# The first expert unit, two tiles of the first four batches, computed block by block between the closing steps of attention

## The chip, the cores and the metric

One core of a Trainium2 chip runs the kernel. The metric is device time in microseconds, the median of three runs.

## The reference

Sparse attention over 8 batches, 8 heads and 576 tokens with 64 values a head (`scores` are scaled by 1/8; all but a row's 32 largest are dropped), then a mixture of 8 experts over the 4608 tokens, each sent to one expert:

```
scores = scale * np.matmul(q, k.transpose(0, 1, 3, 2))
kth = np.partition(scores, -top_k, axis=-1)[..., -top_k:-top_k + 1]
attn = softmax(np.where(scores >= kth, scores, -1e9))        # top_k = 32
x = (attn @ v).transpose(0, 2, 1, 3).reshape(4608, 512)
e = argmax(x @ w_gate)                                       # 8 experts
out[token] = gate[token] * (relu(x[token] @ w1[e]) @ w2[e])  # 512 -> 1024 -> 512
```

## The kernel before, in words

**Attention** runs in 144 steps, one for a group of query rows, in a loop whose count goes to 150 because a step's stages lag: at loop count t the search for the 32nd largest (`topk`, DVE MAX8 and MATCH_REPLACE) works on step t, `softmax` (POOL adds, ACT signs) on step t-2, `transp` (PE transposes into the PSUM tile `tt`) on t-3, `exps` (ACT exponential out of `tt`) and `av` (PE, product with V) one loop count later. For t from 144 on there is no more search; these are the closing steps. Beside the steps run *jobs*, generators in lanes with due times, that advance as a step has room: preparing K and Q, summing and repairing rows (`sums`, `find`, `redo`, `patch`), writing a batch's rows to `xs` and its router logits to `lps` (`rows`), and routing a batch (`route`, `j_route`): it reads the logits `ll`, finds each token's expert (`hist`, `cum`, a rank by PE), and scatters token numbers and gate weights into `table`, whose slots start at `ebase`. In j_route, a batch after which an expert's early unit may be formed (`ahead`) also counts by PE how many slots are missing (`skip`), so that later tokens are put behind that unit's slots, and loads the unit's `ids`.

**Experts.** A *unit* is an expert and a number T of tiles of 128 tokens. `EARLY = ((4, 1, 2), (3, 4, 3))` lists early units: expert 0 with two tiles, from batches 0 to 4; experts 1 to 4 with three, from batches 0 to 5. Experts 5 to 7 have five tiles each, then come the remainders of the early ones and one spare tile. A unit has 8 blocks of 128 hidden values; block k loads raw w1 and w2 slices (`raw_w`), splits each into a high and a low part (`parts_w`: the high copy of w1 on ACT, that of w2 on DVE, the subtraction for w1 on DVE, for w2 on POOL), and runs `hidden(k)` (three products a sum: high by high, high by low, low by high) and `project(k-1)`. `turn_x` transposes a gathered tile into `xh` and `xl`. After a unit's last block ACT scales the sums with the gate weights and POOL sends the rows to `out` with one indirect store a tile.

Ahead of its end, attention already loads blocks 0 and 1 into buffers of the Q and K loads (`rq`, `rk`), gathers unit 0's two tiles (into `kt`) and splits both blocks; everything else of unit 0 comes after the last step: `moe()` begins with unit 0's `turn_x` and goes through all blocks in order, while the jobs of the last batches are advanced between them.

`MAIN` is 4, so `NB9` is 9 chunks of 128 columns; `tt` is then 1152 columns in three banks of 512. `ps` is the two-bank tile of the scores. `sb` are score buffers in SBUF, `qk0` to `qk2` the transposed Q and K.

Of the kernel before, what the change touches and what calls it, by code (L numbers as in the profile page):

```python
# [8 lines left out]
F32 = mybir.dt.float32  # L9
F32R = mybir.dt.float32r  # L10
# [13 lines left out]
CHUNKS = (11, 10)  # L24
A0, A1, A2, A3 = -4, 1, 2, 2
EARLY = ((4, 1, 2), (3, 4, 3))
LA = 3
# [11 lines left out]
TAIL = 1  # L39
TADV = 5  # L40
FREE = (1, 2, 3, 4, 5)
# [7 lines left out]
def attention_moe(ctx, tc, q, k, v, w_gate, w1, w2, out):  # L49
# [134 lines left out]
    def pair():  # L184
        return work.tile([128, 2, S], F32, name="sb", bufs=SBUFS)
# [114 lines left out]
    NB9 = 2 * MAIN + 1  # L300
    three = psum.tile([128, NB9 * 128], F32, name="tt")

# [154 lines left out]
    def transp(t):  # L457
        x = EX[t].rearrange("p a s -> p (a s)")
        tt = three.rearrange("p (c q) -> p c q", c=NB9)
        for c in range(NB9):  # L460
            nc.tensor.matmul(tt[:, c], x[:, c * 128:(c + 1) * 128], ident, start=True, stop=True,  # L461
                             is_transpose=True)

    def exps(t):
        ET[t] = work.tile([128, NB9, 128], F32, name="et")
        assert t // NT in SHIFTED
        nc.scalar.activation(ET[t], three.rearrange("p (c q) -> p c q", c=NB9), AF.Exp, bias=shift[:, t // NT, 0:1],  # L467
                             scale=0.125)
# [320 lines left out]
    def j_route(b):  # L789
# [158 lines left out]

    def parts_w(k, tiles):
        W[k] = []  # L950
        for i, r in enumerate(RAW.pop(k)):
            hi, lo = tiles[2 * i:2 * i + 2]
            if i == 0:
                nc.scalar.activation(hi, r, AF.Copy)  # L954
            else:
                nc.vector.tensor_copy(hi, r)  # L956
            (nc.gpsimd if i else nc.vector).tensor_tensor(lo, r, hi, op=OP.subtract)  # L957
            W[k] += [w.rearrange("p (c f) -> p c f", c=DC) if i == 0 else w for w in (hi, lo)]


    def ahead_load(k):
        r = work.tile([128, MAIN, 4, D], F32, name=("rq", "rk")[k], bufs=1).rearrange("p i g d -> p (i g d)")
        raw_w(k, r[:, 0:DM], r[:, DM:2 * DM])

    def ahead_take():
        c, T = part_of[0]
        GX[0] = [jobs.tile([128, DM], F32, name="kt", bufs=4)[:, 0:DM] for _ in range(T)]
        for i in range(T):
            take(GX[0][i], ID[0][:, i, 0:1], c)

    def ahead_split(k):
        if k == 0:
            for i in range(2):
                t = jobs.tile([128, 2, VW], F32R, name=f"rv{(NQ + i) % NV}", bufs=1).rearrange("p g x -> p (g x)")
                SPARE.extend(t[:, c * DM:(c + 1) * DM] for c in range(2 * VW // DM))
            SPARE.extend(jobs.tile([128, DM], F32, name="kt", bufs=4).bitcast(F32R)[:, 0:DM] for _ in range(2))
        parts_w(k, [SPARE.pop(0) for _ in range(4)])

    SPARE = []
    prep(0)  # L980
# [16 lines left out]
    if NQ > 1:  # L997
        load_qk(1)
    load_v(0)
    prep(2)  # L1000
    AHEAD = [(A0, ahead_load, (0,)), (A0, ahead_load, (1,)), (A1, ahead_take, ()), (A2, ahead_split, (0,)),
             (A3, ahead_split, (1,))]
    delayed = None
    for t in range(steps + LAG + TD + 4):
# [60 lines left out]
        for at, job, a in AHEAD if first else ():  # L1065
            if t - steps == at:
                job(*a)
        m = t - LAG - TD - 3
# [12 lines left out]
    att_open[0] = False  # L1081
    while first and part_of[0][0] not in ROUTED or held[0]:
        advance(None)
        for queue in (gq, pq, aq, dq):
            flush(queue)
# [5 lines left out]
    ps_a = moe_pools.enter_context(tc.tile_pool(name="ps_a", bufs=1, space=PSUM, reuse_waits="tile"))  # L1091
    late = {}
    XP, HT, PY = {}, {}, {}
    outs = []

    def pool_of(u):
        return moe_a if u < first else late["sb"]
# [28 lines left out]

    def turn_x(u, t):
        T = units[u][2]
        if t >= T:
            return  # L1130
        p = pool_of(u)
        if t == 0:
            XP[u] = [p.tile([128, DC, T * 128], F32R, name=n, bufs=2) for n in ("xh", "xl2")]
        xh, xl = XP[u]
        s = slice(t * 128, (t + 1) * 128)
        pt = ps_a.tile([128, DC, 128], F32, name="mt") if u or not t else \
            ps_a.tile([128, 512], F32, name="ph", bufs=2).rearrange("p (c x) -> p c x", c=DC)
        for c in range(DC):
            nc.tensor.transpose(pt[:, c, :], GX[u][t][:, c * 128:(c + 1) * 128], ident)  # L1139
        nc.scalar.activation(xh[:, :, s], pt, AF.Copy)  # L1140
        nc.vector.tensor_tensor(xl[:, :, s], pt, xh[:, :, s], op=OP.subtract)

    def hidden(k):
        u, f = divmod(k, FC)
        T = units[u][2]
        xh, xl = XP[u]
        h1, l1 = W[k][0:2]
        p = pool_of(u)
        hh = p.tile([128, T * 128], F32R, name="hh", bufs=2)
        hl_ = p.tile([128, T * 128], F32R, name="hl", bufs=2)  # L1150
        HT[k] = (hh, hl_)
        nh = 1 if T <= 4 else 2
        w = T * 128 // nh
        for n in range(nh):
            s = slice(n * w, (n + 1) * w)
            ph = ps_a.tile([128, 512], F32, name="ph", bufs=2)[:, 0:w]
            seq = [(c, a, x) for c in range(DC) for a, x in ((h1, xh), (h1, xl), (l1, xh))]
            for m, (c, a, x) in enumerate(seq):
                nc.tensor.matmul(ph, a[:, c, :], x[:, c, s], start=(m == 0), stop=(m == len(seq) - 1))  # L1159
            nc.scalar.activation(hh[:, s], ph, AF.Relu)  # L1160
            nc.vector.scalar_tensor_tensor(hl_[:, s], ph, 0.0, hh[:, s], op0=OP.max, op1=OP.subtract)  # L1161

    def project(k):
        u, f = divmod(k, FC)
        T = units[u][2]
        hh, hl_ = HT.pop(k)
        h2, l2 = W.pop(k)[2:4]
        for t in range(T):
            if f == 0:
                p = ps_a if t < 3 else late["ps"]  # L1170
                PY[u, t] = p.tile([128, DM], F32, name=f"y{t}")
            s = slice(t * 128, (t + 1) * 128)
            for m, (a, x) in enumerate(((hh, h2), (hh, l2), (hl_, h2))):
                nc.tensor.matmul(PY[u, t], a[:, s], x, start=(f == 0 and m == 0), stop=(f == FC - 1 and m == 2))  # L1174
        if f == FC - 1:
            for t in range(T):
                y = pool_of(u).tile([128, DM], F32, name="yo", bufs=3 if u < first else 5)
                nc.scalar.activation(y, PY[u, t], AF.Copy, scale=ID[u][:, t, 2:3].bitcast(F32))  # L1178
                nc.gpsimd.memset(spacer, 0.0)
                st = nc.gpsimd.indirect_dma_start(  # L1180
                    out=out, out_offset=bass.IndirectOffsetOnAxis(ap=ID[u][:, t, 1:2], axis=0),
                    in_=y, in_offset=None, bounds_check=N - 1, oob_is_err=False)
                for o in outs:
                    tc.declare_no_dep(st.ins, o.ins, reason="each token has a row of its own")
                outs.append(st)

    def moe():
        K = len(units) * FC
        got, turned = set(), set()

# [4 lines left out]

        for k in range(2):
            load_w(k)
        while first == 0 and not late:
            yield
        if first:  # L1200
            got.add(0)
        fetch(0)
        load_w(2)
        if not first:
            split_w(0)
            split_w(1)
        for t in range(CT):
            turn_x(0, t)
        turned.add(0)
        for k in range(K):  # L1210
            u, f = divmod(k, FC)
# [10 lines left out]
            split_w(k + 2)  # L1222
            if k:
                project(k - 1)
# [272 lines left out]
```

## Time and profile before

| | us |
|---|---|
| median of 3 runs | 1303.01 (1302.87 to 1304.35) |
| profiled execution | 1301.19, its span 1299.4 |
| PE busy | 1217.2 (94%) |
| DVE busy | 1020.2 (79%) |
| ACT, POOL busy | 828.3 (64%), 830.7 (64%) |
| mean granted TensorE clock | 0.983 of full |

The page divides the span into 40 slices of 32.5 us and gives each engine's busy share in tenths; in the row of the granted clock two slices near 750 to 810 us stand below their neighbours, and DVE's row falls there from 9 to lower digits, where attention ends. A table by stretch gives the same for any two times. A timeline lists each instruction or run of like instructions with its start, its length, and in brackets how long its engine sat idle before it and what ended that. A line number is that of the kernel before; L265 is the helper through which all jobs record.

### The profile page before, as it was taken

The page shows a single profiled execution, that of the slowest core. Times are in us where ns is not written, and L with a number is a line of the kernel's source. Part 1 is how long each engine was busy: PE and PEld are TensorE (multiplying, and loading weights), DVE is VectorE, ACT ScalarE, POOL GpSimd, SP SyncE. Part 2 cuts the span into 40 slices and gives each one's busy share as a digit, 9 for nine tenths or more (in the row PEclk, how much of TensorE's full clock was granted, in tenths as well). Part 3 has the DMA queues.
Part 4 walks back from the last instruction along what each step waited for, and adds up shares of the span by engine and source line. Part 5 has one row for each costly group of instructions (what it writes and reads, how often), then busy time and mean ns, then how long its engine had stood idle before and what let it go on. Part 6 is the DMA issues. An engine that isn't in the chain of part 4 may idle for free.

```text
span 1299.4 us, 31672 instructions
## 1 busy us (share of the span) xinstructions
PE 1217.2 (94%) x9126; PEld 968.9 (75%) x9126; DVE 1020.2 (79%) x6889; ACT 828.3 (64%) x1691; POOL 830.7 (64%) x1205
## 2 busy tenths in 40 slices
PE   6999999999999999999998869999999999999997
PEld 3667667676666666667666658889899899989996
DVE  7999999999999999999998965746663333345664
ACT  4999798898888888888987843333332323233432
POOL 4676766867867867868957866676552424155654
PEclk8999999999999999999999978999999999999999
DMA  6765565655655656556653615646563434256774
GB/s 174 224 184 178 169 187 161 186 171 160 193 161 156 195 168 171 179 170 171 188 166 113 194 39 159 187 122 199 146 184 110 125 93 132 74 162 189 224 212 125
DMA packets 271239, 211.18 MB, mean 163 GB/s; under 512 B 136216, under 2 KB 214216, under 8 KB 271056
## 3 DMA queue, kind: packets, MB, share of 16 engines
q1 hardware_dynamic: 260320, 185.92, 48.2%
q0 software_dynamic: 9504, 22.86, 5.6%
q8 instruction: 74, 1.21, 0.4%
q14 instruction: 109, 0.89, 0.2%
q10 hardware_dynamic: 1232, 0.30, 0.1%
HBM read 102.49 MB, written 107.90 MB: 162 GB/s over the span
## 4 chain that ended last, share of the span: by engine, by line
DVE 43%; PE 43%; ACT 4%; issue 3%; POOL 3%; DMA 2%; SPq 1%; POOLq 0%; ACTq 0%; DVEq 0%
DVE cand L1025 21%; PE ph L1159 18%; PE y L1174 17%; DVE cand L1033 9%; DVE vq L1033 7%; PE pt L265 2%; ACT sg L454 2%; POOL sb L455 2%; PE mt L1139 1%; PE ps L367 1%; PE px L477 1%; PE tt L461 1%; DVE xm L265 1%; ACT et L467 1%; DMA rk<-in_k_dram 1%
## 5 line engine op out<-in xcount | busy, mean ns | idle before, releaser
L455 POOL TENSOR_TENSOR sb<-sb,sg 128x576 f32<-128x576 f32 x288 | 369.4, 1299 | 49.4 <-ACT sg L454 42.3
L1025 DVE MAX8 cand<-sb 128x8 f32<-128x52 f32 (+2 forms) x3024 | 368.3, 207 | 0.2 <-issue 0.2
L957 POOL TENSOR_TENSOR wl<-r,wh 128x512 fp32r<-128x512 f32 x110 | 142.4, 1294 | 220.8 <-DVE wh L956 213.5
L454 ACT ACTIVATE sg<-sb,nb 128x576 int8<-128x576 f32 x288 | 229.0, 795 | 63.0 <-POOL sb L455 63.0
L477 PEld LDWEIGHTS px<-et,rv 128*64 128x64 f32 x2688 | 130.9, 138 | 123.1 <-ACT xt L265 49.4
L1160 ACT ACTIVATE hh<-ph 128x320 fp32r<-128x320 f32 (+3 forms) x136 | 58.2, 428 | 241.6 <-PE ph L1159 240.1
L1033 DVE MAX8 vq<-cand 128x8 f32<-128x22 f32 (+7 forms) x1152 | 200.5, 205 | 0.0
L461 PE MATMUL tt<-turner,sb 128*128 128x128 f32 x1296 | 176.8, 278 | 23.0 <-POOL sb L455 19.9
L367 PE MATMUL ps<-qk 64*128 64x512 f32 (+1 forms) x576 | 184.9, 650 | 4.2 <-ACT sb L369 3.5
L1161 DVE SCALAR_TENSOR_TENSOR hl<-ph,hh 128x320 fp32r<-128x320 f32 (+3 forms) x136 | 65.0, 478 | 151.3 <-ACT hh L1160 151.2
L467 ACT ACTIVATE et<-tt,shift 128x1152 f32<-128x1152 f32 x144 | 178.2, 1238 | 2.6 <-PE tt L461 2.6
L477 PE MATMUL px<-et,rv 128*64 128x128 f32 (+1 forms) x2688 | 164.3, 268 | 14.6 <-ACT xt L265 9.0
L461 PEld LDWEIGHTS tt<-turner,sb 128*128 128x128 f32 x1296 | 147.9, 144 | 34.7 <-POOL sb L455 30.2
L1159 PE MATMUL ph<-xh,wh 128*128 128x320 f32 (+3 forms) x536 | 168.5, 314 | 0.0
L1159 PE MATMUL ph<-xh,wl 128*128 128x320 f32 (+3 forms) x536 | 165.3, 308 | 0.0
L1159 PE MATMUL ph<-xl,wh 128*128 128x320 f32 (+3 forms) x536 | 165.1, 308 | 0.0
L1033 DVE MATCH_REPLACE8 cand<-vq,cand 128x22 f32<-128x22 f32 (+2 forms) x864 | 158.6, 189 | 0.0
L369 ACT ACTIVATE sb<-ps 128x1024 f32<-128x1024 f32 x144 | 149.0, 1035 | 9.4 <-PE ps L367 9.4
L1174 PE MATMUL y<-wh,hh 128*128 128x512 f32 x324 | 127.9, 395 | 1.9 <-ACT yo L1178 1.9
L1174 PE MATMUL y<-wh,hl 128*128 128x512 f32 x324 | 128.3, 396 | 0.0
L1174 PE MATMUL y<-wl,hh 128*128 128x512 f32 x324 | 128.1, 395 | 0.0
L957 DVE TENSOR_TENSOR wl<-r,wh 128x512 fp32r<-128x512 f32 x110 | 95.7, 870 | 11.4 <-ACT wh L954 7.1
(261 smaller groups left out, 2179.3 us busy)
## 6 DMA issues: line engine op xcount, KB each, us to landing
r<-in_moe_w_dram SPq DMA_DIRECT2D x220, 256.0 KB
sc<-sb SPq DMA_DIRECT2D x128, 288.0 KB
sc<-sb SPq DMA_DIRECT2D x128, 256.0 KB
rv<-in_v_dram SPq DMA_DIRECT2D x32, 256.0 KB
xs<-xm SPq DMA_DIRECT2D x16, 512.0 KB
rq<-in_q_dram SPq DMA_DIRECT2D x60, 128.0 KB
rk<-in_k_dram SPq DMA_DIRECT2D x60, 128.0 KB
sc<-sb SPq DMA_DIRECT2D x32, 144.0 KB
```

Of the source, the lines that this page charges most:

```text
L367: nc.tensor.matmul(MAINS[:, n], qk[:, 0, w], qk[:, 1, 2 * LEFT:], start=True, stop=True)
L369: nc.scalar.activation(bass.AP(EX[-1].tensor, EX[-1].offset, [list(EX[-1].ap[0]), [S + LEFT, 2], [1, M]]), MAINS, AF.Copy)
L454: nc.scalar.activation(upper(SG[i]), SB[u], AF.Sign, bias=nb[:, i, 1:2], accum_out=CNT[b][:, 2 * lt + i:2 * lt + i + 1])
L455: nc.gpsimd.tensor_tensor(SB[u], SB[u], SG[i], op=OP.add)
L461: nc.tensor.matmul(tt[:, c], x[:, c * 128:(c + 1) * 128], ident, start=True, stop=True, is_transpose=True)
L467: nc.scalar.activation(ET[t], three.rearrange("p (c q) -> p c q", c=NB9), AF.Exp, bias=shift[:, t // NT, 0:1], scale=0.125)
L477: yield lambda kb=kb, blk=blk: nc.tensor.matmul(px[h * 64:(h + 1) * 64], block(rv, p % 2, kb if kb < MAIN else MAIN + n, h), et[:, blk, q] ...
L957: (nc.gpsimd if i else nc.vector).tensor_tensor(lo, r, hi, op=OP.subtract)
L1025: one[m][0](*one[m][1])
L1033: f(*a)
L1159: nc.tensor.matmul(ph, a[:, c, :], x[:, c, s], start=(m == 0), stop=(m == len(seq) - 1))
L1174: nc.tensor.matmul(PY[u, t], a[:, s], x, start=(f == 0 and m == 0), stop=(f == FC - 1 and m == 2))
```

## The change

Unit 0 now takes its two tiles from the first four batches (0 to 3), a batch earlier; expert 1 becomes a unit of two tiles from batches 0 to 4, and experts 2 to 4 keep three from batches 0 to 5. The number of tiles and the list of unit sizes stay, in another order. All of unit 0 is taken out of `moe()`, which starts at unit 1 (block 8), and goes into a generator `filler()`. It is called once at the end of each of the loop counts 140 to 144, for the loads, gathers, splits and transposes, and from count 145 on once a step, between `softmax` and `av`, for one block: hidden(k), project(k-1), the split of block k+2, the load of block k+4. What is left of it runs behind the loop. Its buffers are those of the scores: the split weights lie in `qk0` to `qk2` and score buffers, x and the hidden values in score buffers, the y sums in `ps`, the hidden sums in the 384 columns by which `tt` is widened. All of its subtractions run on DVE. `TADV`, the number of closing counts in which the jobs advance, goes from 5 to 7. Batch 3 has become a batch with `skip`, and its five table scatters keep their spacing.

```
-EARLY = ((4, 1, 2), (3, 4, 3))
+EARLY = ((5, 1, 2), (4, 1, 2), (3, 3, 3))
-TADV = 5
+TADV = 7
...
-    three = psum.tile([128, NB9 * 128], F32, name="tt")
+    three = psum.tile([128, 3 * 512], F32, name="tt")
...
-            if c == 0 or b not in ahead:
+            if c == 0 or b not in ahead or b == part_of[0][0]:
                 yield need(pool=1.0)
...
+    def filler():
+        T = units[0][2]
+        w = T * 128
+        for k in range(2):
+            ahead_load(k)
+        yield
+        yield
+        ahead_take(0, "kt", DM)
+        yield
+        flat = [work.tile([128, 2, KW], F32, name=f"qk{i}", bufs=1).rearrange("p g x -> p (g x)") for i in range(3)]
+        sets = [halves(flat[0]) + halves(flat[1])]
+        parts_w(0, sets[0], nc.vector)
+        ahead_load(2)
+        XP[0] = [spare().bitcast(F32R)[:, 0:DC * w].rearrange("p (c x) -> p c x", c=DC) for _ in range(2)]
+        hs = spare().bitcast(F32R)
+        yield
+        for t in range(T):
+            turn_x(0, t, MAINS[:, t].rearrange("p (c x) -> p c x", c=DC))
+        sets.append(halves(flat[2]) + halves(spare()))
+        parts_w(1, sets[1], nc.vector)
+        ahead_load(3)
+        yield
+        ph = three[:, NB9 * 128:NB9 * 128 + w]
+        for k in range(FC):
+            h = hs[:, (k % 2) * 2 * w:(k % 2 + 1) * 2 * w]
+            hidden(k, (h[:, 0:w], h[:, w:2 * w], ph))
+            if k:
+                project(k - 1, MAINS)
...
+                parts_w(k + 2, sets[(k + 2) % 3], nc.vector)
...
+            if k + 4 < FC + 2:
+                ahead_load(k + 4)
+            if k >= FC - 3 and 1 not in GX and part_of[1][0] in ROUTED:
+                ahead_take(1, "xt", S)
+            yield
+        while part_of[1][0] not in ROUTED:
+            yield
+        if 1 not in GX:
+            ahead_take(1, "xt", S)
+        project(FC - 1, MAINS, spare())
...
+        if t > steps:
+            next(fills, None)
         if grp(t - LAG - TD - 2):
             av(t - LAG - TD - 2, grp(t - LAG - TD - 2))
...
+        if steps + A0 <= t <= steps:
+            next(fills)
...
-        for k in range(K):
+        for k in range(FC, K):
```

**PE, behind the search's last steps.** Before: from the rank of a batch's route (`hist`, `cum`) through av of steps 140 and 141 (the first two `px<-et` rows; `rv` is V) to the transposes of step 143.

```order
L265 MATMUL pt0_246<-hist_121,before_104 128x40
L265 MATMUL pt0_246<-cum_13209,ones_108 128x40
L477 MATMUL px_250<-et_13287,rv3_240 64x128 x8
L461 MATMUL tt_248<-turner_102,sb_12896 128x128 x9
L265 MATMUL pt0_246<-turner_102,r_sb_12616 128x128 x4
L477 MATMUL px_250<-et_13351,rv3_240 64x128 x8
L461 MATMUL tt_248<-turner_102,sb_12978 128x128 x9
```

The same place now. L978 are the transposes of `turn_x` (`kt` is a gathered tile), L1001 the matmuls of `hidden`, L1016 those of `project`.

```order
L265 MATMUL pt1_247<-hist_121,before_104 128x40
L265 MATMUL pt1_247<-cum_13215,ones_108 128x40
L978 MATMUL ps_249<-turner_102,kt_13216 128x128 x4
L978 MATMUL ps_249<-turner_102,kt_13217 128x128 x4
L1001 MATMUL tt_248<-sb_13308,qk0_13298 128x256
...
L477 MATMUL px_250<-et_13312,rv3_240 64x128 x8
L461 MATMUL tt_248<-turner_102,sb_12902 128x128 x9
L265 MATMUL pt1_247<-turner_102,r_sb_12622 128x128 x4
L1001 MATMUL tt_248<-sb_13308,qk2_13300 128x256
...
L1016 MATMUL ps_249<-qk1_13299,sb_13310 128x512 x6
L477 MATMUL px_250<-et_13396,rv3_240 64x128 x8
```

The transposes of unit 0 and hidden(0) have come between `cum` and av of step 140, hidden(1) and project(0) between av of steps 140 and 141.

**ACT, from unit 0 to unit 1.** In the changed kernel, with the queues and engines that each row waits for (DMASW are POOL's DMAs). L1002 writes the hidden values, L1021 the two scaled output tiles, L979 the copies `xh` of the next unit.

```order
L1002 ACTIVATE sb<-tt 128x256 [waits DVE_49,PE_49]
L954 ACTIVATE rv_13776<-rq 128x512 [waits DMAHW0_49]
L1002 ACTIVATE sb<-tt 128x256 [waits DVE_49,PE_49]
L954 ACTIVATE rv_13777<-rk 128x512 [waits DMAHW2_49]
L1021 ACTIVATE sb<-ps,ids_11146 128x512 [waits PE_49]
L1021 ACTIVATE sb<-ps,ids_11146 128x512
L979 ACTIVATE xh<-mt 128x4x128 [waits DMASW0_49,DMASW7_49,PE_49,Activation_49]
L979 ACTIVATE xh<-ph 128x4x128 [waits PE_49]
L1002 ACTIVATE hh<-ph 128x256 [waits DMAHW7_49,DVE_49,PE_49]
```

In the kernel before, the last outputs of unit 0 (L1178) stand behind a block of unit 1, and unit 1's copies (L1140) behind PE alone.

```order
L1140 ACTIVATE xh<-mt 128x4x128 [waits PE_49]
...
L1140 ACTIVATE xh<-mt 128x4x128 [waits PE_49]
...
L1160 ACTIVATE hh<-ph 128x256 [waits DVE_49,PE_49]
L954 ACTIVATE wh_13958<-r_13897 128x512 [waits DMAHW0_49]
...
L1160 ACTIVATE hh<-ph 128x384 [waits PE_49,Activation_49]
L954 ACTIVATE wh_13995<-r_13954 128x512 [waits DMAHW4_49]
L1178 ACTIVATE yo<-y_13634,ids_12353 128x512 [waits DMAHW3_49,PE_49]
L1178 ACTIVATE yo<-y_13638,ids_12353 128x512 [waits PE_49]
```

What moved: the copies of the next unit, which stood ahead of unit 0's last blocks, now stand behind unit 0's outputs and wait for two of POOL's DMAs; these are the two indirect stores of those outputs.

## Rows read from the trace of the kernel before

**Rows 1.** Stretch, us, busy us of PE, PEld, DVE, ACT, POOL; clock, DMA share, GB/s

```profile
762.00:786.00 24.00, 18.88 (x131) 15.38 (x131) 9.14 (x31) 9.29 (x18) 19.05 (x32) 0.77 0.26 67
```

**Rows 2.** The same view in shorter stretches, for the granted clock

```profile
770.00:776.00 6.00, 5.55 (x32) 4.98 (x33) 0.24 (x2) 2.74 (x7) 5.14 (x11) 0.50 0.32 88
...
788.00:794.00 6.00, 5.77 (x26) 5.64 (x27) 1.67 (x5) 1.36 (x4) 0.92 (x1) 0.53 0.37 116
```

**Rows 3.** Timeline of PE, closing steps: start, us, engine line op out<-in xcount [idle <-releaser]

```profile
761.77 0.23 PE L265 MATMUL pt<-hist,before 128*128 128x40 bf16 x1 [3.05 <-DVE hist L265]
...
762.40 1.97 PE L477 MATMUL px<-et,rv 128*64 128x128 f32 x16
...
770.45 1.97 PE L477 MATMUL px<-et,rv 128*64 128x128 f32 x16 [3.13 <-ACT r_et L265]
...
785.35 0.35 PE L265 MATMUL pt<-rhs,r_qx 128*128 128x2 bf16 x8 [1.73 <-DVE r_qx L265]
```

**Rows 4.** Timeline of DVE, same columns: the split of a block

```profile
775.87 0.69 DVE L957 TENSOR_TENSOR rv<-rq,rv 128x512 fp32r<-128x512 f32 x1 [5.76 <-ACT rv L954]
776.48 0.42 DVE L956 CAST rv<-rq 128x512 fp32r<-128x512 f32 x1
```

**Rows 5.** Timelines of ACT and POOL: an exponential, a gather

```profile
762.61 1.21 ACT L467 ACTIVATE et<-tt,shift 128x1152 f32<-128x1152 f32 x1
...
770.95 1.09 POOL L876 DMA_INDIRECT kt<-xs,ids  x1 [0.16 <-issue]
```

**Rows 6.** Timeline of PE: the first unit's blocks and what follows

```profile
785.59 0.63 PE L1139 MATMUL mt<-turner,kt 128*128 128x128 f32 x4
...
788.23 0.58 PE L1159 MATMUL ph<-xl,rv 128*128 128x256 f32 x1 [0.25 <-DVE xl L1141]
...
793.31 0.81 PE L1174 MATMUL y<-rv,hh 128*128 128x512 f32 x2
...
794.88 0.90 PE L265 MATMUL pt<-turner,xt 128*128 128x144 f32 x6
...
795.96 0.36 PE L1159 MATMUL ph<-xh,wh 128*128 128x256 f32 x1
...
797.48 0.63 PE L1174 MATMUL y<-kt,hh 128*128 128x512 f32 x2
...
817.17 0.33 PE L1159 MATMUL ph<-xh,wh 128*128 128x384 f32 x1
...
820.66 0.33 PE L1159 MATMUL ph<-xh,wh 128*128 128x384 f32 x1
...
824.82 0.50 PE L1174 MATMUL y<-wh,hh 128*128 128x512 f32 x1 [1.91 <-ACT yo L1178]
```

**Rows 7.** Timeline of ACT: xh, a wait for weights, two outputs

```profile
786.26 0.60 ACT L1140 ACTIVATE xh<-mt 128x512 fp32r<-128x512 f32 x1 [0.35 <-PE mt L1139]
...
823.56 0.63 ACT L954 ACTIVATE wh<-r 128x512 fp32r<-128x512 f32 x1 [3.26 <-DMA r<-in_moe_w_dram]
824.10 1.25 ACT L1178 ACTIVATE yo<-y,ids 128x512 f32<-128x512 f32 x2
```

**Rows 8.** All indirect stores of output rows: durations in ns, times to landing

```profile
L1180 POOL DMA_INDIRECT out_dram<-yo,ids x41: 981/1006/1452, 828.6 to 1291.9; - x41
...
DMA to landing us min/median/max: 2.6/3.7/6.0
```

**Rows 9.** Timelines around skip: DVE and PE at batch 4, both where batch 3's goes

```profile
706.66 0.16 DVE L265 TENSOR_SCALAR skip<-pt 128x1 f32<-128x1 f32 x1 [4.43 <-ACT sg L454]
...
707.37 0.57 DVE L265 TENSOR_TENSOR ebase<-ebase,skip 128x5 f32<-128x5 f32 x1
...
698.06 2.57 PE L461 MATMUL tt<-turner,sb 128*128 128x128 f32 x9 [4.66 <-POOL sb L455]
...
631.81 0.96 PE L265 MATMUL pt<-wg,r_et 128*128 128x8 f32 x8
...
634.24 0.17 DVE L1033 MATCH_REPLACE8 cand<-vq,cand 128x22 f32<-128x22 f32 x1
```

More of the change, by code (lines that the diff above doesn't have):

```diff
@@ L947, in raw_w, with parts_w @@
             nc.sync.dma_start(r2, w2[e, f * 128:(f + 1) * 128, :])
-    def parts_w(k, tiles):
+    def parts_w(k, tiles, other=None):
         W[k] = []
@@ L956, in parts_w, with turn_x @@
                 nc.vector.tensor_copy(hi, r)
-            (nc.gpsimd if i else nc.vector).tensor_tensor(lo, r, hi, op=OP.subtract)
+            ((other or nc.gpsimd) if i else nc.vector).tensor_tensor(lo, r, hi, op=OP.subtract)
             W[k] += [w.rearrange("p (c f) -> p c f", c=DC) if i == 0 else w for w in (hi, lo)]
+    late = {}
+    XP, HT, PY = {}, {}, {}
+    outs = []
+    def turn_x(u, t, pt=None):
+        T = units[u][2]
+        if t >= T:
+            return
+        if u not in XP:
+            p = pool_of(u)
+            XP[u] = [p.tile([128, DC, T * 128], F32R, name=n, bufs=2) for n in ("xh", "xl2")]
+        xh, xl = XP[u]
+        s = slice(t * 128, (t + 1) * 128)
+        if pt is None:
+            pt = ps_a.tile([128, DC, 128], F32, name="mt") if u > 1 or not t else \
+                ps_a.tile([128, 512], F32, name="ph", bufs=2).rearrange("p (c x) -> p c x", c=DC)
+        for c in range(DC):
+            nc.tensor.transpose(pt[:, c, :], GX[u][t][:, c * 128:(c + 1) * 128], ident)
+        nc.scalar.activation(xh[:, :, s], pt, AF.Copy)
+        nc.vector.tensor_tensor(xl[:, :, s], pt, xh[:, :, s], op=OP.subtract)
@@ new lines, in hidden @@
+    def hidden(k, tiles=None):
+        u, f = divmod(k, FC)
+        T = units[u][2]
+        xh, xl = XP[u]
+        h1, l1 = W[k][0:2]
+        if tiles:
+            hh, hl_, _ = tiles
+        else:
+            p = pool_of(u)
+            hh = p.tile([128, T * 128], F32R, name="hh", bufs=2)
+            hl_ = p.tile([128, T * 128], F32R, name="hl", bufs=2)
+        HT[k] = (hh, hl_)
+        nh = 1 if T <= 4 else 2
+        w = T * 128 // nh
+        for n in range(nh):
+            s = slice(n * w, (n + 1) * w)
+            ph = tiles[2] if tiles else ps_a.tile([128, 512], F32, name="ph", bufs=2)[:, 0:w]
+            seq = [(c, a, x) for c in range(DC) for a, x in ((h1, xh), (h1, xl), (l1, xh))]
+            for m, (c, a, x) in enumerate(seq):
+                nc.tensor.matmul(ph, a[:, c, :], x[:, c, s], start=(m == 0), stop=(m == len(seq) - 1))
+            nc.scalar.activation(hh[:, s], ph, AF.Relu)
+            nc.vector.scalar_tensor_tensor(hl_[:, s], ph, 0.0, hh[:, s], op0=OP.max, op1=OP.subtract)
@@ new lines, in project @@
+    def project(k, py=None, ys=None):
+        u, f = divmod(k, FC)
+        T = units[u][2]
+        hh, hl_ = HT.pop(k)
+        h2, l2 = W.pop(k)[2:4]
+        for t in range(T):
+            if f == 0:
+                PY[u, t] = py[:, t] if py is not None else \
+                    (ps_a if t < 3 else late["ps"]).tile([128, DM], F32, name=f"y{t}")
+            s = slice(t * 128, (t + 1) * 128)
+            for m, (a, x) in enumerate(((hh, h2), (hh, l2), (hl_, h2))):
+                nc.tensor.matmul(PY[u, t], a[:, s], x, start=(f == 0 and m == 0), stop=(f == FC - 1 and m == 2))
+        if f == FC - 1:
+            for t in range(T):
+                y = ys[:, t * DM:(t + 1) * DM] if ys is not None else \
+                    pool_of(u).tile([128, DM], F32, name="yo", bufs=3 if u < first else 5)
+                nc.scalar.activation(y, PY[u, t], AF.Copy, scale=ID[u][:, t, 2:3].bitcast(F32))
+                nc.gpsimd.memset(spacer, 0.0)
+                st = nc.gpsimd.indirect_dma_start(
+                    out=out, out_offset=bass.IndirectOffsetOnAxis(ap=ID[u][:, t, 1:2], axis=0),
+                    in_=y, in_offset=None, bounds_check=N - 1, oob_is_err=False)
+                for o in outs:
+                    tc.declare_no_dep(st.ins, o.ins, reason="each token has a row of its own")
+                outs.append(st)
@@ L968, in ahead_take @@
         for i in range(T):
[L969 to L977, printed above, removed]
@@ L1081, in attention_moe @@
     att_open[0] = False
-    while first and part_of[0][0] not in ROUTED or held[0]:
+    while held[0] or next(fills, fills) is not fills:
         advance(None)
@@ L1125, in gather @@
             take(GX[u][t], ID[u][:, t, 0:1], part_of[u][0] if u < first else None)
[L1127 to L1185, printed above, removed]
@@ L1187, in moe @@
     def moe():
         K = len(units) * FC
-        got, turned = set(), set()
+        got, turned = {0, 1}, {0}
         def fetch(u):
@@ L1194, in fetch @@
                 gather(u)
[L1196 to L1209, printed above, removed]
-        for k in range(K):
+        load_w(FC + 2)
+        for k in range(FC, K):
             u, f = divmod(k, FC)
```

43 lines of the change are left out of this document (26 added, 17 removed).

## The prediction

> **What bounds the kernel now.** I read the page's slices first, then a table by stretch, then the timelines of the single engines between the end of attention and the second expert unit. Until about 760 us DVE works without a pause on the top-32 search, and every DVE microsecond added there is added to the time. From 821 us to the end PE is the bound. Between the two lies the closing stretch, 762 to 786 us: PE is busy for 18.88 of 24 us, at a mean granted clock of 0.77 [rows 1]. So 5.1 us of PE stand idle there and the rest is partly slow. The idle time comes from waits: 3.05 us for hist, 3.13 us for r_et, 1.73 us for r_qx [rows 3]. Each is followed by a stretch at 0.50, the lower of TensorE's two levels, 1.2 GHz: 770 to 776 us directly after the wait for r_et, and 788 to 794 us at 0.53 [rows 2]. What the change can win is those 5.1 us and part of the slow clock. After the last patch matmul (the "mark" from here on, r_qx at 785.35) the first unit's eight blocks run: block 0's hidden layer from 788.23, and the whole unit is finished with the second unit's first block at 820.66 [rows 6].
>
> **What a block costs.** Two hidden layers at the half clock take 788.23 to 793.31, 2.55 us each; one at full clock takes 795.96 to 797.48, 1.5 us. A projection is six matmuls at 0.23 us, 1.4 us (797.48 to the next entry) [rows 6].
>
> **Part 1, main stage.** Batch 3 is now a batch whose routing also adjusts the slot base: one small matmul, three DVE operations, one 4 KB load. The load and the matmul lie beside other work. The DVE operations do not: 0.16 and 0.57 us and one as short as the first [rows 9], together 0.8 us after pipelining, on the engine that sets the time. At batch 4 the first of them also waited 4.43 us, because PE was late that step: it had itself waited 4.66 us for POOL. At batch 3's place PE has just finished the logits matmuls at 631.81 to 632.8, and DVE reaches the spot where skip is inserted at 634.4, so the operand is there before it [rows 9]. The bounds are 0.6 and 5 us; I take **+0.8**, the row nearest in place.
>
> **Part 2, the start of the closing stretch.** The split of block 0 is now on DVE ahead of hist: 0.61 us to the cast, 0.34 for it, 0.6 for the second subtraction (starts in [rows 4]), 1.55 us. PE's hist goes from 761.77 to about 763.3, its sum to 764.2. PE then does unit 0's transposes before av(140). Four transposes at the slow clock take 0.9 us, the copy xh 0.6 [rows 7], the subtraction 0.7; the second tile's transposes wait for the first tile's subtraction, because both lie in the one PSUM tile that the scores used. Twice 2.2 is 4.4 us: 768.6. ACT comes to the exponential of step 141 (1.21 us [rows 5]) only after both copies, so it ends near 769.5. Block 0's hidden sums go to the last third of the tile that this exponential reads, so hidden(0) starts at 769.5 and at half clock ends at 772.1. Only then comes av(140), which stood at 762.40 [rows 3]: **9.7 us late**. The two gathers of unit 0, 1.09 us of POOL each [rows 5], move into the last steps of attention, two steps ahead of what POOL's sums feed; I cost that at nothing, and at most 2.2 us if that lead is gone.
>
> Here a rule speaks for the wait. The trace has PE waiting 3.13 us for ACT to empty a tile that shares its bank with another job's output [rows 3]. The Trainium skill, "PSUM — Partial Sum Buffer", section "PSUM bank collisions raise a hardware error", says that two engines may not touch one bank and quadrant together even at different columns, so the exponential has to be out of the bank before hidden(0) begins; by columns alone hidden(0) would start 0.9 us sooner and the sum would be that much lower. The row agrees.
>
> **Part 3, to the mark.** From av(140) to the mark the kernel before needs 785.35 - 762.40 = 23 us with its 5.1 us of idle PE. The changed order puts hidden(1), (2), (3) and project(0), (1), (2) in between: 3 x 1.5 + 3 x 1.4 = 8.7 us at full clock. If these fill all the idle time the mark comes at 772.1 + 23 + 8.7 - 5.1 = **798.7**. I take neither a gain from a faster clock nor a loss from the further waits (each hidden layer waits for that step's exponential, each exponential for the splits of the step before); these have opposite signs. Bounds: were all of PE's added work, 10.2 us of blocks and 0.9 of transposes, laid into the holes and the slow stretch raised to full clock (18.88 x 0.23 = 4.3 us), the mark would be at 785.35 + 11.1 - 5.1 - 4.3 = 787. With the same six pieces at half clock (3 x 2.55 + 3 x 2.6 = 15.5) it would be 772.1 + 23 + 15.5 - 5.1 = 805.5.
>
> **Part 4, the rest of unit 0.** Behind the mark: four hidden layers and five projections, 6.0 + 7.0, and the patch jobs' matmuls between them. Before, 795.96 to 817.17 holds six hidden layers and six projections (17.4), three transposes of 0.43 and so 2.5 us of such jobs, and 1.08 us more stand at 794.88 [rows 6]: 3.6 us. The unit ends at 798.7 + 16.6 = 815.3.
>
> **Part 5, the hand-over, a new wait.** Unit 0's two output tiles are put into a score buffer, and the area where unit 1's xh lies covers it. Unit 1's first copy on ACT therefore waits for both indirect stores of the output. After project(7): one scaled copy 0.65 (two take 1.25 [rows 7]), some 0.3 to POOL's issue, 1.3 for the first store (1.0 us and its gap [rows 8]), then the second to landing 3.7 (median; 2.6 to 6.0 [rows 8]), two xh copies 1.0, one subtraction 0.7: **7.7 us** in which PE has nothing but the two transposes and what is queued behind them. hidden(8) begins at 823.0. Only by a page's figure: the Trainium skill, "DMA: Bandwidth & Descriptors", section "Anatomy of one DMA", gives about 2.0 us and the bytes over 436 GB/s, an estimate of 2.6 us for 256 KB, and the sum would be 1.1 us lower; the trace's least landing is that, its median is not [rows 8].
>
> Then TensorE falls to its lower level, as it did after 3.1 us of idling [rows 2, 3]. Priced by the stretch at 0.53: 6 x 0.47 = **2.8 us**.
>
> **Against the kernel before.** There 820.66 is reached with hidden(8) done (2.1 us, from 817.17) and about one transpose set more, so the same work lies behind it at 818.1. Behind that stood 1.91 us at 824.82, for weights whose load sat on SP behind a load of router logits (ACT waits 3.26 us for them [rows 6, 7]). In the changed kernel these weights have 7.7 idle microseconds to arrive, so this stall goes: 820.0 is to be compared. Difference: 823.0 - 820.0 + 2.8 + 0.8 = +6.6. Everything behind is the same number of tiles in units of the same sizes. The profiled execution took 1301.19 and so 1307.8 now; it lies 1.8 below the median of 1303.01, on which the forecast stands: 1309.6, given as **1309.5**.
>
> DVE has 9.14 of 24 us filled [rows 1]; eight splits of 1.55 over the 40 us of the unit do not make it the bound. The lanes that patch and route the last batches end later, at block 31 of 40, and the spare units still find their tokens.
>
> **Rivals.** A difference below 0.2%, 2.6 us, cannot be told from none here.
> *The holes are filled* (faster): PE's early blocks keep it from idling, the clock stays at its upper level through the closing stretch and the mark comes at 787 to 788. Then the sum is 11 lower: 1298.5. For it: 5.1 us of idle PE and a clock of 0.77. Against: the chains of single operations across PE, ACT and DVE in part 2, which put more waiting ahead of av(140). It decides where the mark lies ahead of about 789. Chance 0.13.
> *Half of it* (no change): the mark at 792 to 794, or the hand-over paid without a drop of the clock; 1302 to 1305. Chance 0.20.
> *Nothing overlaps* (slower still): each hidden layer waits for an exponential that waits for a split, the blocks run as a second string at the lower clock, and the mark stands at the upper bound of 805.5: 6.8 more, 1316.3. Chance 0.12.
> *skip stalls at batch 3 as at batch 4*: 4.4 us more, 1314. Against it stand the times of rows 9. Chance 0.08.
> The forecast, 1306 to 1313, keeps 0.47.
>
> **The numbers.** Slower is 0.47 + 0.12 + 0.08 = 0.67, same 0.20, faster 0.13. The range leaves out the far half of the faster case and the end of the one in which nothing overlaps: 1301 to 1316.
>
> **What would show it.** The mark (r_qx matmuls) near 798; av(140) ten microseconds later than before; a wait of PE on xh or on its transposes' copy of 6 to 7 us near 815 to 823, named by a DMA of the output, and a clock near 0.5 right behind it; no wait for weights at the second unit; skip's three operations near 634 without a wait. Wrong would be: a mark ahead of 790, PE at full clock from 762 to 786, a hand-over below 3 us, or DVE idle for microseconds before 757.

## The result and the profile after

The changed kernel takes 1314.63 us (median of 4 runs, 1313.59 to 1317.0), the kernel before 1302.94 on the same chips (1300.34 to 1304.35). The ratio is 1.0095 with a 95% interval of 1.0074 to 1.0116: 11.7 us slower, where 6.5 had been forecast. The profiled execution took 1317.0 with a span of 1314.7 and is the longest of the four.

The closing stretch by the same table as [rows 1]: start and end, length, busy us of PE, PE's weight loads, DVE, ACT and POOL, then the granted clock, DMA share and GB/s.

```profile
762.00:786.00 24.00, 13.35 (x89) 10.90 (x88) 15.54 (x45) 8.97 (x17) 10.64 (x16) 0.72 0.22 68
786.00:821.00 35.00, 33.16 (x241) 28.22 (x240) 17.28 (x38) 10.26 (x22) 19.79 (x36) 1.00 0.57 146
```

PE is not busier from 762 to 786 but less busy, 13.35 us against 18.88, and the clock is 0.72 against 0.77. DVE is busier, 15.54 against 9.14. Only the stretch behind it, 786 to 821, is better: a clock of 1.00 against 0.90 before.

The timeline of PE, as in [rows 3, 6]. The first line, the transposes of rinvl, is the last work of the search's steps.

```profile
761.55 0.35 PE L265 MATMUL pt<-rinvl,turner 128*64 128x1 f32 x8
766.76 0.23 PE L265 MATMUL pt<-hist,before 128*128 128x40 bf16 x1 [4.87 <-DVE hist L265]
...
773.28 2.93 PE L1001 MATMUL tt<-sb,qk 128*128 128x256 f32 x12 [2.31 <-ACT et L467]
776.14 1.97 PE L477 MATMUL px<-et,rv 128*64 128x128 f32 x16
...
801.38 0.34 PE L265 MATMUL pt<-rhs,r_qx 128*128 128x2 bf16 x8
...
816.94 1.66 PE L1016 MATMUL ps<-sb 128*128 128x512 f32 x6
...
826.85 0.58 PE L1001 MATMUL ph<-xh,rv 128*128 128x256 f32 x1 [7.38 <-ACT xh L979]
...
832.69 0.62 PE L1016 MATMUL y<-rv,hh 128*128 128x512 f32 x2
```

In the kernel before the same instruction stood here:

```profile
758.37 0.35 PE L265 MATMUL pt<-rinvl,turner 128*64 128x1 f32 x8
```

All of PE's closing work is best counted from that line. The changed profile lies 3.18 us later at it (761.55 against 758.37). From there av(140) comes 14.6 us later, at 776.14, where it came 4.0 us later before (762.40 [rows 3]); the mark 39.8 us later (801.38) instead of 27.0; unit 0's last projection (it starts at 816.94) gives way to unit 1's transposes at 818.44, 56.9 us behind that line. Then PE stands for 7.38 us and starts unit 1 at 826.85, and the first two hidden layers there take until 832.69, 5.84 us instead of 3.0.

The table by stretch between these places, first the kernel before (rinvl to av(140), av(140) to the mark), then the changed one:

```profile
758.37:762.40 4.03, 0.72 (x14) 0.46 (x10) 3.96 (x20) 0.49 (x3) 2.31 (x3) 0.65 0.06 13
762.40:785.35 22.95, 18.09 (x119) 14.73 (x118) 8.59 (x28) 9.12 (x17) 18.00 (x32) 0.76 0.25 66
```

```profile
761.55:776.14 14.59, 5.67 (x34) 4.52 (x30) 9.62 (x29) 4.73 (x10) 5.74 (x5) 0.59 0.19 55
776.14:801.38 25.24, 23.09 (x172) 18.67 (x172) 12.76 (x34) 8.60 (x16) 13.54 (x28) 0.96 0.43 106
```

Ahead of av(140) PE now stands idle for 8.9 us (14.59 - 5.67) instead of 3.3. Behind it, up to the mark, it is idle for 2.2 us instead of 4.9 and runs at 0.96 of the clock instead of 0.76. So the blocks did fill the holes behind av(140), but larger ones opened ahead of it.

The waits of PE from 740 us to the end (what waited, for what, us in total, how often, the longest):

```profile
PE tt L1001 <- ACT et L467: 4.2, 2, 2.3
PE y L1016 <- DVE hl L1003: 3.2, 1, 3.2
...
PE mt L978 <- DMA gx<-xs,ids: 1.8, 2, 1.5
```

The first belongs to hidden(0) and hidden(1), which wait for an exponential. The other two lie behind unit 0: 3.2 us for hl at 953, and 1.8 for the gathered tiles of unit 2.

ACT and POOL at the hand-over:

```profile
818.63 1.26 ACT L1021 ACTIVATE sb<-ps,ids 128x512 f32<-128x512 f32 x2 [3.15 <-PE ps L1016]
825.71 0.60 ACT L979 ACTIVATE xh<-mt 128x512 fp32r<-128x512 f32 x1 [5.81 <-DMA out_dram<-sb,ids]
```

```profile
820.97 0.97 POOL L1023 DMA_INDIRECT out_dram<-sb,ids  x1 [0.21 <-issue]
```

The second store was issued at 820.97 and xh could be written at 825.71, 4.7 us later; ACT's row names the stores as what ended its wait.

The second stall comes at the plan of the spare tile (the small operations that make the table of the last tiles), a place that the prediction did not price. POOL, DVE and PE there, and the granted clock behind it:

```profile
945.32 0.99 POOL L876 DMA_INDIRECT gx<-xs,ids  x1
...
951.38 0.19 POOL L1296 IOTA tl_i<- 128x44 f32 x1
```

```profile
951.61 0.19 DVE L1301 TENSOR_SCALAR tr<-tl_i 128x44 f32<-128x44 f32 x1 [7.75 <-issue]
```

```profile
953.23 0.79 PE L1016 MATMUL y<-wh,hl 128*128 128x512 f32 x1 [3.19 <-DVE hl L1003]
```

```profile
950.00:955.00 5.00, 1.81 (x5) 1.49 (x5) 3.25 (x10) 0.62 (x2) 2.07 (x4) 0.71 0.51 155
955.00:960.00 5.00, 5.00 (x20) 4.50 (x20) 3.88 (x11) 0.60 (x1) 1.74 (x2) 0.61 0.57 161
```

POOL issues the five gathers of a five-tile unit from 945.32 on, and only then the iota that the plan starts from (951.38). DVE stands idle for 7.75 us; its row names no releaser, but the operation reads what the iota writes and starts as that ends (951.57). The hl of a block is queued behind it; PE waits 3.19 us for that hl, and runs ten microseconds at 0.71 and 0.61. In the kernel before the same operation of DVE waited 0.21 us:

```profile
927.25 0.19 DVE L1261 TENSOR_SCALAR tr<-tl_i 128x44 f32<-128x44 f32 x1 [0.21 <-POOL tl_i L1256]
```

DVE in the main stage, a wait and batch 3's skip:

```profile
DVE skip L265 <- PE pt L265: 5.3, 1, 5.3
```

```profile
635.64 0.14 DVE L265 TENSOR_SCALAR skip<-pt 128x1 f32<-128x1 f32 x1
```

skip at batch 3 has no wait, as forecast. The wait for skip at batch 4 is 0.9 us longer than in the profile of before [rows 9]; one for mm (part of a batch's shift), between 100 and 200 us, takes 3.5 us against 1.5. The latter is not the change: in the kernels whose code up to there is that of the changed one it lies anywhere between 1.1 and 3.8 us. The two make up most of the 3.18 us by which this profile is late at the first line.

### The profile page after: what moved, and what is told of

The parts are those of the page before. It is cut to its first block, busy times and chain, and to the rows that moved or that the text cites. A ratio compares the mean times of both kernels' runs of the same rounds, so it can differ in the third digit from the quotient of the medians.

```text
span 1314.7 us, 31668 instructions
## 1 busy us (share of the span) xinstructions
PE 1219.1 (93%) x9127; PEld 968.9 (74%) x9127; DVE 1016.1 (77%) x6902; ACT 827.6 (63%) x1691; POOL 821.6 (62%) x1194
## 4 chain that ended last, share of the span: by engine, by line
DVE 47%; PE 39%; issue 5%; POOL 3%; ACT 3%; DMA 2%; SPq 1%; POOLq 0%; ACTq 0%; DVEq 0%
DVE cand L1143 23%; PE ph L1001 16%; PE y L1016 15%; DVE cand L1151 10%; DVE vq L1151 8%; PE pt L265 2%; PE px L477 1%; PE ps L367 1%; PE mt L978 1%; DVE xm L265 1%; PE tt L461 1%; ACT sg L454 1%; DMA rk<-in_k_dram 1%; ACT et L467 1%; SPq L113 1%
## 5 line engine op out<-in xcount | busy, mean ns | idle before, releaser
L957 POOL TENSOR_TENSOR wl<-r,wh 128x512 fp32r<-128x512 f32 x102 | 131.8, 1293 | 228.2 <-DVE wh L956 220.8
L454 ACT ACTIVATE sg<-sb,nb 128x576 int8<-128x576 f32 x288 | 228.6, 794 | 61.4 <-POOL sb L455 60.5
L1002 ACT ACTIVATE hh<-ph 128x320 fp32r<-128x320 f32 (+3 forms) x128 | 55.2, 431 | 236.2 <-PE ph L1001 225.0
L1003 DVE SCALAR_TENSOR_TENSOR hl<-ph,hh 128x320 fp32r<-128x320 f32 (+3 forms) x128 | 61.6, 481 | 149.5 <-ACT hh L1002 142.1
L1001 PE MATMUL ph<-xh,wh 128*128 128x320 f32 (+3 forms) x504 | 159.3, 316 | 0.0
L1001 PE MATMUL ph<-xh,wl 128*128 128x320 f32 (+3 forms) x504 | 155.8, 309 | 0.0
L1001 PE MATMUL ph<-xl,wh 128*128 128x320 f32 (+3 forms) x504 | 155.8, 309 | 0.0
L1016 PE MATMUL y<-wh,hl 128*128 128x512 f32 x308 | 122.0, 396 | 3.2 <-DVE hl L1003 3.2
L1016 PE MATMUL y<-wl,hh 128*128 128x512 f32 x308 | 121.7, 395 | 0.0
L1016 PE MATMUL y<-wh,hh 128*128 128x512 f32 x308 | 121.1, 393 | 0.0
L1001 PEld LDWEIGHTS ph<-xh,wh 128*128 128x128 f32 x504 | 95.1, 189 | 5.6 <-issue 2.6
```

The costliest lines, as they stand in the source:

```text
L454: nc.scalar.activation(upper(SG[i]), SB[u], AF.Sign, bias=nb[:, i, 1:2], accum_out=CNT[b][:, 2 * lt + i:2 * lt + i + 1])
L957: ((other or nc.gpsimd) if i else nc.vector).tensor_tensor(lo, r, hi, op=OP.subtract)
```

## The experiments

All ratios are against runs of the kernel before on the same chip.

### The outputs of unit 0 in other buffers

```
-                y = ys[:, t * DM:(t + 1) * DM] if ys is not None else \
+                y = ys[t] if ys is not None else \
...
-        project(FC - 1, MAINS, spare())
+        project(FC - 1, MAINS, [jobs.tile([128, DM], F32, name="kt", bufs=4)[:, 0:DM] for _ in range(T)])
```

> The changed kernel with unit 0's two output tiles in two gather buffers that are free by then, so that unit 1's copies no longer wait for the output's stores. Theory (the hand-over costs its wait and a slow clock behind it): PE's wait of 7.4 us for xh falls to under 2 us, the two blocks behind it run at 1.5 us a hidden layer instead of 2.9, and 8 to 9 us come off: about 1306, some 0.2 to 0.4% above the kernel before. Rival (the wait only hides that unit 2's gathers and the next weights are late): the wait comes back as waits for gx or r, and at most 3 us come off, about 1312.

1308.03 us, ratio 1.0045 (1.0029 to 1.006): 0.5% off, some 6.5 us. PE's timeline, and the clock behind the hand-over:

```profile
760.10 0.35 PE L265 MATMUL pt<-rinvl,turner 128*64 128x1 f32 x8
...
819.09 0.38 PE L1001 MATMUL ph<-xh,rv 128*128 128x256 f32 x1 [1.46 <-ACT xh L979]
...
824.27 0.62 PE L1016 MATMUL y<-rv,hh 128*128 128x512 f32 x2
```

```profile
819.00:825.00 6.00, 5.46 (x28) 5.13 (x29) 2.44 (x6) 1.47 (x5) 1.82 (x2) 0.72 0.63 218
```

The wait for xh falls from 7.38 to 1.46 us, as the theory has it. Its second half fails: the two hidden layers still take 5.2 us (819.09 to 824.27, with one wait of 0.45 inside), at a clock of 0.72. That is only 0.66 us less than the 5.84 behind the long wait, so 6.5 us come off where 8 to 9 were expected. The rival is out: the wait for unit 2's gathers is 1.4 us here and 1.8 in the changed kernel.

### The iota of the plan ahead of the gathers

```
+        tl_i = sb.tile([128, MT], F32, name="tl_i")
+        nc.gpsimd.iota(tl_i, pattern=[[1, MT]], base=0, ...)
         nc.vector.memset(cum[:, 0:1], 0.0)
...
         step()
-        tl_i = sb.tile([128, MT], F32, name="tl_i")
-        nc.gpsimd.iota(tl_i, pattern=[[1, MT]], base=0, ...)
```

> The changed kernel with the iota of the spare tile's plan issued ahead of the gathers on POOL. Theory (the plan fell behind a five-tile gather because the jobs ended four blocks later): DVE's 7.75 us at the plan and PE's 3.2 us for hl go, with the clock of 0.61 to 0.71 behind them: 5 to 6 us off, about 1309. Rival (a chance of this one execution, or a wait hidden anyway): under 1 us off, about 1314.

1309.53 us, ratio 1.0052 (1.0034 to 1.007): 5.1 us off.

```profile
PE y L1016 <- DVE hl L1003: 0.5, 1, 0.5
```

PE's wait for hl falls from 3.2 to 0.5 us, DVE's at the plan is gone, and the granted clock is 1.00 from 945 to 960. The theory holds, in its size too.

### Both

> Both edits of the two kernels beside it. If the two waits are separate, the gains add up: 13 to 15 us off, about 1300.5, no more than 0.2% from the kernel before. If one only moves the other's stall, the sum is smaller by the smaller of the two: about 1306.

1303.15 us, ratio 1.0008 (0.9995 to 1.0021). The two gains add up, 6.5 and 5.1 us, and the kernel is where the kernel before was, to within the interval's 2.7 us. It is less than the 13 to 15 us expected, as the first edit alone had given less. So these two waits with the slow clock behind them are the loss, as far as the interval tells, and PE work laid between the closing steps has brought nothing that can be measured. The next runs ask why.

### The blocks behind each step's av and transp

The call of the generator moves behind `transp`; all else is the changed kernel.

```
-        if t > steps:
-            next(fills, None)
         if grp(t - LAG - TD - 2):
             av(t - LAG - TD - 2, grp(t - LAG - TD - 2))
...
             transp(t - LAG - TD)
+        if t > steps:
+            next(fills, None)
```

> The changed kernel with each closing step's block behind that step's av and transp instead of ahead of them. Theory (hidden(0) ahead of av(140) delays the closing chain): av(140) comes some 5 us earlier, hidden layers no longer wait for an exponential (4.2 us), and unit 0 ends 3 to 5 us sooner: about 1310. Rival (PE's work and the jobs set unit 0's end, the order does not matter): within 1 us of 1314.6.

1316.45 us, ratio 1.0097 (1.008 to 1.0115): no gain. PE's timeline, with the last work of the search at 760.69:

```profile
770.34 1.98 PE L477 MATMUL px<-et,rv 128*64 128x128 f32 x16
...
780.45 1.98 PE L477 MATMUL px<-et,rv 128*64 128x128 f32 x16 [4.12 <-ACT r_et L265]
...
800.56 0.35 PE L265 MATMUL pt<-rhs,r_qx 128*128 128x2 bf16 x8
```

av(140) does come 5 us earlier (9.7 us behind that line instead of 14.6), and the waits for exponentials go. But av(141) then waits 4.12 us for r_et, and the mark lies 39.9 us behind the line, as before the edit (39.8), with the same blocks ahead of it. The theory falls: what holds up the mark is not PE's order.

### What ACT does first

ACT, POOL and PE in the run of both edits:

```profile
766.67 0.60 ACT L979 ACTIVATE sb<-ps 128x512 fp32r<-128x512 f32 x1 [0.70 <-PE ps L978]
...
770.28 1.22 ACT L467 ACTIVATE et<-tt,shift 128x1152 f32<-128x1152 f32 x1
...
777.05 0.78 ACT L265 ACTIVATE vq<-vq,shift 128x576 f32<-128x576 f32 x1 [1.64 <-POOL tiny L265]
```

```profile
772.33 2.53 POOL L455 TENSOR_TENSOR sb<-sb,sg 128x576 f32<-128x576 f32 x2 [7.55 <-ACT sg L454]
```

```profile
779.98 1.70 PE L1001 MATMUL tt<-sb,qk 128*128 128x256 f32 x12 [1.84 <-ACT et L467]
```

ACT has the copies of unit 0's x (L979) ahead of the exponential of step 141 and of the last signs (L454). The exponential that ran at 762.61 before [rows 5] runs at 770.28 here, the sign behind it at 771.38, and POOL, idle for 7.55 us, comes to its last two sums at 772.33. The repair chain starts from those sums: it reaches ACT again at 777.05 (vq), the next exponential at 778.72, and for that hidden(1) waits until 779.98. From there PE has no idle time up to the end of unit 0. So I put the first split, the transposes and the copies later, behind the exponential, signs, av and transp of loop count 145, on top of both edits; the blocks follow one step later than before, behind each step's transp (the call between `softmax` and `av` goes, as in the run above):

```
-        if steps + A0 <= t <= steps:
+        if steps + A0 <= t <= steps + A1:
             next(fills)
...
             transp(t - LAG - TD)
+        if t == steps + 1:
+            next(fills)
+        if t > steps:
+            next(fills, None)
```

> Both waits taken away as in the run of both edits, and unit 0's first split, its transposes and copies put one step later, behind that step's exponential, signs, av and transp; the blocks follow behind each step's transp. Theory (ACT and DVE work in order, so copies and a split set ahead of the last exponential and of hist hold up the signs, POOL's last sums and the repair chain): the exponential of step 141 and the last signs come about 8 us earlier, r_key on DVE near 768 to 770 instead of 779, the mark 5 us or more earlier; unit 0 ends 2 to 5 us sooner and the time is 1298 to 1301. Rival (PE's work and the slow clock set unit 0's end whatever the order): within 1.5 us of 1303.

1300.69 us, ratio 0.9990 (0.9981 to 1.0). The same views:

```profile
764.40 1.22 ACT L467 ACTIVATE et<-tt,shift 128x1152 f32<-128x1152 f32 x1
```

```profile
766.45 3.06 POOL L455 TENSOR_TENSOR sb<-sb,sg 128x576 f32<-128x576 f32 x2 [1.90 <-ACT sg L454]
```

And PE, in the run of both edits and in this one, each with the table's row from the end of PE's last wait in unit 0 to unit 0's end:

```profile
759.62 0.35 PE L265 MATMUL pt<-rinvl,turner 128*64 128x1 f32 x8
...
799.09 0.34 PE L265 MATMUL pt<-rhs,r_qx 128*128 128x2 bf16 x8
...
818.63 0.38 PE L1001 MATMUL ph<-xh,rv 128*128 128x256 f32 x1 [1.46 <-ACT xh L979]
```

```profile
779.98:816.14 36.16, 36.16 (x267) 30.83 (x267) 20.36 (x49) 10.02 (x22) 20.91 (x35) 1.00 0.47 139
```

```profile
760.51 0.35 PE L265 MATMUL pt<-rinvl,turner 128*64 128x1 f32 x8
...
794.28 0.35 PE L265 MATMUL pt<-rhs,r_qx 128*128 128x2 bf16 x8
...
816.64 0.38 PE L1001 MATMUL ph<-xh,rv 128*128 128x256 f32 x1 [1.45 <-ACT xh L979]
```

```profile
774.34:814.15 39.81, 39.81 (x278) 34.95 (x279) 23.51 (x59) 12.50 (x27) 21.00 (x39) 0.93 0.48 134
```

Counted from the first line, the exponential comes 6.8 us sooner, the mark moves from 39.5 to 33.8 us and unit 1's start from 59.0 to 56.1: 2.9 us sooner, inside what the theory expected. The mark's 5.7 us overstate the gain: three hidden layers and two projections stand ahead of it here, four and three in the run of both edits, and that block, some 2.9 us, now follows behind the mark. What is gained is PE's idle time ahead of its last wait's end, 6.4 us instead of 10.9, and part of that is given back by a lower clock behind it, 0.93 instead of 1.00. One expectation failed: r_key came at 775.25, not at 768 to 770, behind unit 0's splits on DVE; in neither run did PE wait for what hangs on it. In time it is 0.18%, with intervals that just overlap, so the trace carries this verdict more than the times do.

A smaller edit, again on both, moved only block 0's split from ahead of hist to behind the transposes (`parts_w(0, ...)` and the load behind it go to the end of the `turn_x` loop).

> Both waits taken away, and only block 0's split moved from ahead of hist to behind unit 0's transposes. Theory (the split ahead of hist holds up the chain): PE waits 2 us less for hist, hidden(0) does not come later than now, and up to 2 us come off, about 1301.5. Rival (hidden(0) waits for the split instead): within 1 us of 1303.

1302.98 us, ratio 1.0004 (0.9993 to 1.0015), no difference:

```profile
PE tt L1001 <- ACT et L467: 6.2, 2, 3.4
```

PE waits for hist 2.7 us instead of 5.0, but hidden layers wait 6.2 us for exponentials instead of 4.2. The split's 2 us were not what set the time.

### The list of early units alone

```
-EARLY = ((4, 1, 2), (3, 4, 3))
+EARLY = ((5, 1, 2), (4, 1, 2), (3, 3, 3))
```

> The kernel before with only the new list of early units: batch 3 gets its skip, unit 0 takes from batches 0 to 3, the sizes stand in the new order, and all blocks still run behind attention. Theory of the forecast's part 1: 0.8 us slower, 1303.6, with skip's operations at batch 3 without a wait. Rival (the new order of sizes alone brings the plan behind a five-tile gather): 5 us or more slower, about 1308.

1306.78 us, ratio 1.0037 (1.0024 to 1.0051): 4.9 us slower, about the size that the rival named, but for a reason that neither side had:

```profile
DVE skip L265 <- PE pt L265: 9.5, 2, 4.8
```

DVE waits for skip twice now, 4.7 us at batch 3 and 4.8 at batch 4. The plan's iota stood ahead of the gathers in this run, so the new order of the units alone does not bring the stall at the plan. What differs from the changed kernel is that batch 3's five scatters were issued in one go. The wait at batch 4 shows the same in the changed kernel's own trace, POOL and then PE:

```profile
690.71 1.08 POOL L847 DMA_INDIRECT table<-pay,pos  x1 [2.41 <-DVE vq L1151]
...
698.97 2.51 POOL L455 TENSOR_TENSOR sb<-sb,sg 128x576 f32<-128x576 f32 x2
```

```profile
700.30 2.57 PE L461 MATMUL tt<-turner,sb 128*128 128x128 f32 x9 [4.66 <-POOL sb L455]
```

Five scatters fill POOL from 690.71 to 697; the sums of the scores start at 698.97, PE's transposes wait 4.66 us for them, and the small matmul for skip stands behind on PE. Two more runs spaced scatters out, in the kernel with the new list alone (batch 3's) and in the kernel before (batch 4's), with the clause that the change itself has:

```
-            if c == 0 or b not in ahead:
+            if c == 0 or b not in ahead or b == part_of[0][0]:
```

> The kernel before with the new list of early units and, as in the changed kernel, batch 3's five table scatters spaced out, so that part 1 of the forecast stands by itself. Theory (the 4.9 us of the run with the list alone are a second wait of skip, behind five scatters in one go): skip's wait at batch 3 goes, and the time is 0.8 to 1.5 us over the kernel before, 1302.6 to 1303.5. Rival (the new order of the units costs, not the wait): it stays 3 us or more slower.

1303.71 us, ratio 0.9998 (0.9988 to 1.0007). The wait at batch 3 is gone:

```profile
634.49 0.15 DVE L265 TENSOR_SCALAR skip<-pt 128x1 f32<-128x1 f32 x1
```

The 0.8 us of skip's operations are not seen in the time; at most 0.9 us (the interval's end) fit. The one wait for skip that is left, at batch 4, takes 6.0 us in this profile.

> The kernel before with batch 4's five table scatters spaced out. Theory (POOL's five scatters in one go hold up the sums for the scores, PE's transposes wait 4.66 us for them, and skip on DVE 4.4 us for PE): skip's wait goes and 4 to 4.5 us come off, about 1297.5. Rival (unit 0 then waits for its token list, or another wait takes the place): under 1 us off.

1299.58 us, ratio 0.9968 (0.9954 to 0.9982): 4.2 us off the kernel before, and the profile has no wait for skip left. The theory holds.

### All of it

Both waits taken away, the transposes one step later, and batch 4's scatters spaced as well (`b in (part_of[0][0], part_of[1][0])`):

> The kernel with both waits gone and the transposes one step later, and batch 4's scatters spaced out as well. Theory: skip's wait of 5 us in the main stage goes and the time falls by as much, to about 1296, 0.4 to 0.5% under the kernel before. Rival (the later route of batch 4 holds up unit 1): under 2 us off, 1299 or more.

1298.01 us, ratio 0.9956 (0.9943 to 0.9969), 5.7 us under the kernel before and the lowest ratio of all. Most of that is the spacing, which needs nothing of the change: the kernel before with it stands at 0.9968. The 0.12% between the two is not settled, as their intervals overlap. One wait stays in every kernel with the generator and was not taken up: PE waits 1.9 us for lostb, just ahead of the plan, where it was 0.3 in the kernel before.

## Why the prediction was right in direction and short in size

**The two closing parts held almost to the microsecond, in part by luck.** Taking off the 3.18 us by which the profile is late at the end of attention, the mark lies at 798.2 (forecast 798.7) and unit 0 ends at 815.3 (forecast 815.3). hist came at 763.6 instead of 763.3, and av(140) at 773.0 instead of 772.1. From there to the mark, two terms that the forecast had put at nothing cancel: 2.2 us of idle time stayed, and PE was busy for 23.1 us, not for the 18.1 of before and 8.7 of blocks, as its clock was 0.96 and no longer 0.76. The forecast had named both and their signs, not their sizes. A hidden layer at the lower level took 2.9 us (773.28 to 776.14), not 2.55, which was read from 788.23, behind that layer's first matmul at 787.40. Its 5.1 us of idle time were also put down in part to the wait for hist, which ends at 761.77, ahead of the stretch from 762; it is ahead of av(140) that the change added idle time.

**But the reason given for the mark was only half of it.** The prediction saw the exponential behind both copies on ACT, but followed it only to hidden(0) and from there to av(140), the order on PE. The run with the blocks behind av and transp shows that this order does not set the mark. The traces point to the copies' place on ACT, ahead of the last exponential and signs, and so of POOL's sums and the repair chain. Moving them later, with the split and the blocks, brought unit 0's end 2.9 us forward; the split alone, on both edits, and the blocks alone, on the changed kernel, gave nothing. The copies alone were not moved, so their part is shown by the trace and by what is left, not by a run of its own.

The bank rule of the Trainium skill, "PSUM — Partial Sum Buffer", section "PSUM bank collisions raise a hardware error", was weighed at 0.9 us. The trace agrees that hidden(0) waits for the exponential, 2.31 us, though it writes other columns. What the rule costs is not shown: in the run without these waits another one, 4.12 us for r_et, took their place, and the time stayed.

**The hand-over** was forecast at 7.7 us and took 8.4 (818.44 to 826.85): from the start of the second store's issue it was 4.7 us until the buffer was free, not the median's 3.7 [rows 8], and from there to hidden(8) 1.1 us, not 1.7. The estimate of 2.6 us from "DMA: Bandwidth & Descriptors" of the Trainium skill, section "Anatomy of one DMA", is further off here. Without the wait, and the little of the slow clock that goes with it, 6.5 us come off. **The slow clock** behind it was forecast at 2.8 us and measured at 2.84 (5.84 against 3.0), but its price does not hang on the long wait: behind one of 1.46 us 2.2 of it stay.

**The main stage** was forecast at +0.8 us; the run that has this part alone gives -0.3, between -1.6 and +0.9.

**The step that failed**, though the direction held, is "Everything behind is the same number of tiles in units of the same sizes", with "The lanes that patch and route the last batches end later, at block 31 of 40, and the spare units still find their tokens". The later end was seen and costed at nothing. It moves the plan of the spare tile on POOL behind the gathers of a five-tile unit, and this costs 5.1 us, which is nearly the whole distance between the forecast's 6.5 and the measured 11.7. **A smaller miss** is the stall for weights: it went as forecast, 1.91 us, but waits for unit 2's gathers of 1.8 us came in its place. They do not hang on the hand-over: 1.4 us of them stay without it.

None of the rivals came as a whole. The first, filled holes, was right behind av(140), where idle time fell from 4.9 to 2.2 us and the clock rose; ahead of it idle time rose by 5.6 us, which is what the rival's counter-argument had said of the chains across PE, ACT and DVE.

## What to carry to other kernels

When work of one stage is laid into another's closing steps, look first at the engines that turn its operands around in order (here ACT), since a copy that waits for something new holds up everything of the old chain behind it. When a stage's end moves, follow also the small one-off steps that hang on it to their new place and read what stands ahead of them on each queue. A buffer that a store still reads is a wait until the store has landed, 4.7 us here, for whoever writes there next; a free one elsewhere gave back half of the loss.

## What the runs showed of the hardware beyond what was expected

PE ran slowly behind the hand-over even where it had waited only 1.46 and 0.45 us: clock 0.72 from 819 to 825, against 0.53 behind the wait of 7.38 us.

```profile
827.00:833.00 6.00, 5.75 (x26) 5.41 (x27) 2.08 (x5) 1.01 (x3) 0.52 (x1) 0.53 0.00 0
```

Five indirect DMAs in one go held POOL for over 6 us in both places shown (690.71 to 697, 945.32 to 951.38), and the wait was passed on to an engine that reads nothing of them: from POOL to PE and on to DVE in the first, from POOL to DVE and on to PE in the second.
